# Attention with head mixing on one core: T's place and A become two tiles, and the first two units' odd heads are sent from ScalarE's queue

## The chip, the cores and the metric

One core of a Trainium2 chip runs the whole program. The metric is the device time of one execution in microseconds, as the median of three runs. The engines go by the names of the profile: PE (TensorE), with PEld its weight loads, DVE (VectorE), ACT (ScalarE), POOL (GpSimd) and SP (SyncE, which here only begins transfers).

## What is computed

An attention layer whose heads are mixed before and after the softmax, and behind it a dense layer with a gated activation.

```python
scores = scale * np.matmul(q, k.transpose(0, 1, 3, 2))       # 4 batches, 12 heads, 448 x 448, head size 64
scores = np.einsum('bhij,hg->bgij', scores, w_pre)
scores = scores - np.max(scores, axis=-1, keepdims=True)
attn = np.exp(scores)
attn = attn / (np.sum(attn, axis=-1, keepdims=True) + 1e-09)
attn = np.einsum('bhij,hg->bgij', attn, w_post)
x = np.matmul(attn, v)                                       # to (1792, 768)
h = x @ w_in                                                 # to (1792, 2048)
g = h * np.clip(h + 3.0, 0.0, 6.0) / 6.0
out = g @ w_out                                              # to (1792, 768)
```

## The kernel before

Query rows are worked through in 32 units of 60 rows, eight to a batch (the last of a batch holds fewer). One unit `m` goes through these stations:

- **Scores.** PE multiplies queries by keys for two pairs of heads at a time (L432, `p` = 0, 1, 2). The result is copied from PSUM to a tile `s`: by ACT in one piece (L457), or in the first two units by ACT for the even heads and by DVE for the odd ones (L454, L455).
- **Regrouping.** Mixing heads on PE needs the heads along the partitions. So for each head one transfer (L464) takes its 60 rows of 448 numbers from `s` to a tile `T`, as 10 partitions times 6 rows, 105 KB. A unit has twelve. All are begun on SP's queue. `T` of the even units lies in the columns 0 to 5375 of a large tile `AR`, that of the odd units in a tile of its own, `T_one`.
- **Steps.** Three steps a unit, each with up to 20 query rows: mix before the softmax (PE, L521), row maximum (DVE, L529), exponent with row sum (ACT, L530), a small sum on POOL (L532) and its reciprocal on DVE (L533), normalisation (POOL, L539), the split of a number into two halves of 16 bits (ACT, L541, and POOL, L542), and the mix after the softmax (PE, L558). Its two PSUM results go to `A`, one by ACT (L569) and one by DVE (L567). `A` is the part of `AR` from column 6144 on, a ring of three units.
- **Values.** PE multiplies `A` by the values (L603), and ACT and DVE write `x` (L608, L609).
- **Dense layer, first half.** L801 with the activation L814 and L816, for every group of 240 or 208 rows; `g` goes to memory and comes back later. The weights are read and decoded meanwhile: `w_in` by L649 to L719 from transfers of 768 KB (L341), `w_out` likewise.
- **Phase B.** When attention is done, `AR` is used again for weights and for `g` of the second half (L898, L899; two slots of 11520 columns, `wg`), and the products L1071 run to the end.

The order of all this on each engine is drawn up by a planner in the kernel (`Plan`). Every operation is entered with its engine, a planned duration, what it reads and writes and a due time. The planner plays the program through with these durations, for several small variations of the due times, keeps the shortest and emits the instructions in that order. Where PE has a planned gap between 9 and 150 us it puts in multiplications of no use (`filler`, L839), to keep the clock up. The planner treats `T` and `A` as separate buffers. The waits between engines come from elsewhere: the framework records which tiles an instruction touches and puts in semaphore waits for them. Transfers take turns on eight semaphores, so that each also waits for the landing of the one eight places earlier; the rows of order below name these DMAHW0 to DMAHW7.

Of the kernel before, what the change touches and what calls it, by code (L numbers as in the profile page):

```python
# [11 lines left out]
F16 = mybir.dt.float16  # L12
BF16 = mybir.dt.bfloat16
F32 = mybir.dt.float32
# [9 lines left out]
B, H, S, D = 4, 12, 448, 64  # L24
DM, FF = 768, 2048
NT = B * S
P = 128
# [4 lines left out]
CU = 60  # L32
# [259 lines left out]
def body(ctx: ExitStack, tc: tile.TileContext, q4, kT, vj, wpre0, wpost0, ident0, w_in, w_out, outT):  # L292
    nc = tc.nc
    PE, ACT, DVE, POOL, SP = nc.tensor, nc.scalar, nc.vector, nc.gpsimd, nc.sync
# [4 lines left out]
    apool = ctx.enter_context(tc.tile_pool(name="apool", bufs=1))  # L299
# [9 lines left out]
    plan = Plan()  # L309
# [3 lines left out]
    def buf(pool, shape, dt, tag, name, bufs=1, ring=True):  # L313

        g = rings.setdefault((id(pool), tag), Ring(bufs)) if ring else None
        return Buf(lambda: pool.tile(shape, dt, tag=tag, name=name, bufs=bufs), g)

    def const(shape, dt, name, pool=keep):
        return Buf(lambda: pool.tile(shape, dt, name=name))

    def act(dur, fn, r, w, prio):
        return plan.op("ACT", dur, fn, r, w, prio)

    def dve(dur, fn, r, w, prio, share=False):
        return plan.op("DVE", dur, fn, r, w, prio, share=share)
# [4 lines left out]
    def pe(dur, fn, r, w, prio, after=(), mode=0):  # L330
        return plan.op("PE", dur, fn, r, w, prio, after, 0, mode)

    def dma(nbytes, fn, r, w, prio, after=()):
        return plan.op("SP", 0.5, fn, r, w, prio, after, nbytes)
# [22 lines left out]
    def place(places):  # L357
        z = Buf(None)
        z.pool = places
        return z  # L360
# [50 lines left out]
        qs[b, c] = t  # L411
        (bulk if b + c else dmas)(P * QX * 4, t, q4[b, c], [t], at, after)

    AR = const([P, 23424], F16, "AR", apool)
    T_one = const([P, 6, S], F32, "T_one", one)
    T_home = [lambda: AR()[:, :5376].bitcast(F32).rearrange("p (t j) -> p t j", t=6), T_one]
    T_zero = [Buf(None), T_one]
    a_ring = Ring(3)
    last_qk, last_av, Ts, Au = [], [], {}, {}

    def a_view():
        return AR()[:, 6144:].bitcast(F32).rearrange("p (x y) -> p x y", y=3 * CU)

    def products(q, half, ks_, p, at):

        def mm():
            for cc in range(2):
                pr = 2 * p + cc
                o = (6 * half + pr) * CU
                for u in range(2):  # L430
                    r = slice(u * D, u * D + D)
                    PE.matmul(at[u]()[cc * D:cc * D + D], q()[r, o:o + D], ks_[cc]()[r, pr % 3, :], start=True, stop=True)  # L432

        return mm

    def scores(m, p, at):
        b, n = divmod(m, 8)
        c, half = divmod(n, 2)
        if p == 0:
            Ts[m] = Buf(T_home[m % 2], rings.setdefault(("T", m % 2), Ring(1)))  # L440
        T, q = Ts[m], qs[b, c]
        ks_ = [ks[b, (2 * p + cc) // 3] for cc in range(2)]
        kr = [(ks_[cc], (2 * p + cc) % 3) for cc in range(2)]
        st = buf(wpool, [P, 2, S], F32, "x", f"s_{m}_{p}", X_BUFS) if m == 0 else buf(rot, [P, 2, S], F32, "s", f"s_{m}_{p}", 2)
        if m < 2 and (m or p):
            ps = [place(singles) for u in range(2)]
            at2 = [lambda u=u: ps[u]()[:, :S] for u in range(2)]
        else:
            two = place(pairs)
            ps = [(two, 0), (two, 1)]  # L450
            at2 = [lambda u=u: two()[:, u, :S] for u in range(2)]
        last_qk[:] = [pe(0.77, products(q, half, ks_, p, at2), [*kr, q], ps, at, last_qk, mode=1)]
        if m < 2:
            act(0.48, lambda: ACT.activation(st()[:, 0], at2[0](), AF.Copy), [ps[0]], [(st, 0)], at + 0.5)  # L454
            dve(0.57, lambda: DVE.tensor_copy(st()[:, 1], at2[1]()), [ps[1]], [(st, 1)], at + 0.5)  # L455
        else:
            act(0.9, lambda: ACT.activation(st(), two()[:, :, :S], AF.Copy), ps, [(st, 0), (st, 1)], at + 0.5)  # L457
        parts = [(0, 10, 6, 0)] if n < 7 else [(0, 10, 2, 0), (20, 5, 2, 2)]
        for cc in range(2):
            for u in range(2):  # L460
                h = 2 * (2 * p + cc) + u
                for q0, r, t, t0 in parts:
                    def go(cc=cc, u=u, h=h, q0=q0, r=r, t=t, t0=t0):
                        SP.dma_start(T()[4 + h:4 + h + 12 * (r - 1) + 1:12, t0:t0 + t], st()[D * cc + q0:D * cc + q0 + r * t, u, :])  # L464

                    dma(r * t * 2100, go, [(st, u), T_zero[m % 2]], [(T, (h, t0))], at + 0.7)


    vs = {}
# [32 lines left out]
    def step(s):  # L502
# [31 lines left out]
        if t == 0:  # L534
            Au[m] = Buf(a_view, a_ring)
# [312 lines left out]
    for m in range(2):  # L848
        for p in range(3):
            scores(m, p, -10 + 8 * m + 1.6 * p)  # L850
# [6 lines left out]
    for s in range(NS + 12):  # L857
# [5 lines left out]
        while todo and todo[0][0] - 2 <= s:  # L863
            at, m, p = todo.pop(0)
            if p == 0 and m % 2 == 0:
                queries(m // 8, m % 8 // 2, at - 5)
            scores(m, p, at)
# [13 lines left out]
        for C in range(16):  # L881
            b, c = divmod(C, 4)
# [28 lines left out]
    def minus(out, x, y, op, at, big, after=()):  # L911
        plan.op("DVE", 1.15, lambda: DVE.tensor_tensor(out(), x(), y(), op=op), [x, y], [out], at, after, share=True)

    WS, GP = {}, {}
    wg_ring = Ring(2)

    def wg(i):
        return Buf(lambda: AR()[:, 11520 * i:11520 * i + 11520], wg_ring)

    slots = [wg(i) for i in range(2)]  # L920
    t_last, a_last = last_pre[-5:-2], last_av[-4:]

    def w_view(t, z, i):
        return t()[:, :6144].rearrange("p (z m f c) -> p z m f c", z=2, m=3, f=8)[:, z, i // 2, 4 * (i % 2):4 * (i % 2) + 4]

    def g_view(t, at, z):
        return t()[:, at:at + 1792].rearrange("p (z f n) -> p z f n", z=2, f=4)[:, z]

    WS["P1"] = slots[0]

    def w_split(name, i, t, at, after):
        b = WS[name]
        split(View(t, lambda: t().rearrange("p (f c) -> p f c", f=4)), wo_r[int(name not in ("P1", "P2"))], lambda y: w_view(b, y, i), (b, (name, i)), 4 * P, at, after, False)

    def g_split(name, b, i, t, x, o, at, after):
        GP[name, b, i] = (lambda z: g_view(x, o, z)), (x, (name, b, i))
        split(t, g_s[b], lambda z: g_view(x, o, z), (x, (name, b, i)), 4 * NH, at, after, True)
# [69 lines left out]
    def g_tile(name):  # L1007
        return gbuf([P, 4, NH], F32, "gr", name, GR)

    def g_load(b, kk, half, i, at):  # L1010
        t = g_tile(f"g{kk}{half}_{b}_{i}_{at}")
        src, keys_ = g_rows(b, kk, half, i)
        load(458752, lambda: SP.dma_start(t(), src()), keys_, [t], at, [close_a])
        return t

    def g_put(name, b, i, t, at, home):
        after = [close_a]
        if home is None:
            ring = later_home.pop(0) if name not in ("P1", "P2") and later_home else "gx"
            if ring == "gy":  # L1020
                after = [close_a, close_w]
            x = gbuf([P, 1792], F16, "gx", f"gx_{name}_{b}_{i}", GX) if ring == "gx" else wbuf([P, 1792], F16, "gy", f"gy_{name}_{b}_{i}", GY)
            home = x, 0
        x, o = home
        g_split(name, b, i, whole(t), x, o, at, after + (a_last if x is slots[1] else []))
# [10 lines left out]
    def g_two(b, at):  # L1036
        later_home[:] = ["gy"] * GY
        if b % 2:
            z = [wg(i) for i in range(2)]
        for i in range(2):  # L1040
            t = at + (6 if b else G2_BY) * i
            b12, b11, b22, b21 = g_load(b, 0, 1, i, t), g_load(b, 0, 0, i, t + 0.1), g_load(b, 1, 1, i, t + 0.2), g_load(b, 1, 0, i, t + 0.3)
            t1 = g_tile(f"t1_{b}_{i}")
            minus(t1, b12, b11, ALU.subtract, t + 1, True)
            minus(b11, b22, t1, ALU.subtract, t + 1.1, True)
            minus(b12, b22, b12, ALU.subtract, t + 1.2, True)
            minus(b21, b21, b11, ALU.subtract, t + 1.3, True)
            for j, (name, x) in enumerate((("P6", b11), ("P7", b12), ("P4", b21), ("P5", t1), ("P3", b22))):
                home = None
                if b % 2:  # L1050
                    n = 5 * i + j
                    home = z[n // 5], 1792 * (n % 5)
                g_put(name, b, i, x, t + 2 + j, home)

    u_t = {}
# [78 lines left out]
    for b in range(B):  # L1134
        g_two(b, 2000 + 1000 * b if b else G2_AT)
        stage2(b, 20000 + 1000 * b)
# [54 lines left out]
```

## Time and profile before

| | us |
|---|---|
| median of three runs | 926.43 |
| lowest, highest | 920.86, 934.22 |
| profiled execution | 935.05 |
| its span, first to last instruction | 933.3 |
| PE busy, of the span | 838.6 (90%) |
| DVE, ACT, POOL busy | 602.5, 529.7, 373.1 |
| mean granted clock of PE | 0.936 |

The profile is of one execution. Busy time of PE is modelled at the ends of matmuls, and a matmul at the lower clock is busy for longer. A wait for several semaphores is put down to the one that came last.

### The profile page before, as it was taken

How to read it: one execution, taken by the hardware profiler on the slowest of the kernel's cores; microseconds unless marked ns; L12 is line 12 of the kernel's file. 1: busy time of each engine (PE TensorE's matmuls, PEld its weight loads, DVE VectorE, ACT ScalarE, POOL GpSimd, SP SyncE). 2: the span in 40 equal slices, each digit the busy share in tenths (PEclk: the TensorE clock that was granted, in tenths of full speed). 3: DMA queues.
4: the chain of work that ended last, by engine and by line, in shares of the span. 5: the costliest groups of instructions: out<-in, count | busy, mean ns of one | idle time of the engine just before them, and what ended most of it. 6: DMA issues, size and time to landing. Idle time of an engine off the chain costs nothing.

```text
span 933.3 us, 28114 instructions
## 1 busy us (share of the span) xinstructions
PE 838.6 (90%) x11599; PEld 661.4 (71%) x11599; DVE 602.5 (65%) x1185; ACT 529.7 (57%) x1043; POOL 373.1 (40%) x535
## 2 busy tenths in 40 slices
PE   8699997698798898898897898889899999999998
PEld 2356665455475675676575666567799999999998
DVE  4477584458565734877565597586457588898542
ACT  3357685467676755676666666678447475243110
POOL 3145686267774744565545446668200000000000
PEclk9779699789999998999988999899999999999999
DMA  6563543362534465554645656553449785463301
GB/s 211 187 188 119 157 137 120 93 216 92 176 104 132 120 203 185 173 176 144 196 122 188 199 178 199 173 159 92 122 131 356 221 264 173 124 185 113 100 25 46
DMA packets 100417, 146.98 MB, mean 157 GB/s; under 512 B 9824, under 2 KB 79552, under 8 KB 100288
## 3 DMA queue, kind: packets, MB, share of 16 engines
q1 hardware_dynamic: 100288, 145.17, 50.1%
q8 instruction: 91, 1.49, 0.7%
q14 instruction: 38, 0.31, 0.1%
HBM read 75.23 MB, written 31.20 MB: 114 GB/s over the span
## 4 chain that ended last, share of the span: by engine, by line
PE 51%; DMA 12%; DVE 10%; ACT 8%; SPq 7%; POOL 6%; issue 5%; ACTq 0%; DVEq 0%; POOLq 0%
PE single L1071 21%; PE single L801 13%; SPq L464 6%; DMA AR<-s 6%; PE single L558 5%; PE pair L432 4%; PE single L521 3%; POOL e L539 3%; DVE nb L529 3%; POOL el L542 3%; PE single L603 2%; ACT e L530 2%; ACT s L457 2%; DMA T_one<-s 2%; DMA wsd_P<-WF 2%
## 5 line engine op out<-in xcount | busy, mean ns | idle before, releaser
L801 PEld LDWEIGHTS <-wi 128*128 128x128 f16 x2304 | 217.3, 99 | 37.1 <-issue 28.9
L801 PE MATMUL single<-x,wi 128*128 128x208 f16 (+1 forms) x2304 | 233.3, 263 | 9.4 <-ACT AR L569 6.6
L542 POOL TENSOR_TENSOR el<-e,eh 128x448 f16<-128x448 f32 x156 | 172.3, 1119 | 87.9 <-ACT eh L541 85.6
L539 POOL TENSOR_SCALAR e<-e,r 128x448 f32<-128x448 f32 x180 | 132.2, 746 | 77.1 <-DVE r L533 69.7
L1071 PEld LDWEIGHTS <-ws_P 128*128 128x128 f16 x1440 | 138.0, 98 | 0.0
L530 ACT ACTIVATE e<-single,nb 128x448 f32<-128x448 f32 x180 | 113.0, 637 | 35.2 <-DVE nb L529 34.9
L432 PE MATMUL pair<-ks,qx 64*64 64x448 f32 x728 | 101.6, 627 | 27.7 <-ACT s L457 27.3
L567 DVE TENSOR_SCALAR AR<-single 128x480 f32<-128x480 f32 (+1 forms) x92 | 58.4, 641 | 95.6 <-DMA AR<-s 68.7
L529 DVE TENSOR_REDUCE nb<-single 128x1 f32<-128x448 f32 x180 | 102.5, 613 | 21.9 <-PE single L521 21.6
L569 ACT ACTIVATE AR<-single 128x480 f32<-128x480 f32 (+1 forms) x92 | 52.9, 582 | 100.1 <-DMA AR<-s 66.5
L457 ACT ACTIVATE s<-pair 128x896 f32<-128x896 f32 x90 | 82.3, 915 | 37.6 <-DMA T_one<-s 20.6
L541 ACT ACTIVATE eh<-e 128x448 f16<-128x448 f32 x156 | 87.0, 576 | 19.8 <-POOL e L539 18.7
L814 ACT ACTIVATE g<-single,three,uh 128x240 f32<-128x240 f32 (+1 forms) x128 | 68.2, 540 | 51.6 <-PE single L801 51.2
L603 PEld LDWEIGHTS single<-AR,v 128*64 128x64 f32 x1536 | 80.6, 144 | 22.5 <-DVE AR L567 6.3
L558 PEld LDWEIGHTS <-eh 60*128 60x128 f16 x2496 | 69.2, 101 | 34.4 <-issue 31.2
L603 PE MATMUL single<-AR,v 128*64 128x120 f32 (+1 forms) x1536 | 86.1, 273 | 6.6 <-DVE AR L567 6.2
L816 DVE SCALAR_TENSOR_TENSOR g<-g,six,single 128x240 f32<-128x240 f32 (+1 forms) x128 | 56.3, 442 | 53.4 <-ACT g L814 53.1
L558 PE MATMUL single<-wpost_h,eh 60*128 60x60 f16 x1248 | 76.6, 204 | 11.1 <-ACT e L530 5.4
L558 PE MATMUL single<-wpost_h,el 60*128 60x60 f16 x1248 | 75.6, 204 | 4.4 <-POOL el L542 4.4
L558 PE MATMUL single<-wpost_l,eh 60*128 60x60 f16 x1248 | 75.4, 204 | 0.0
L1071 PE MATMUL single<-gx_P,ws_P 128*128 128x224 f16 x720 | 69.3, 259 | 0.0
L1071 PE MATMUL single<-AR,ws_P 128*128 128x224 f16 x720 | 69.3, 259 | 0.0
(241 smaller groups left out, 1163.8 us busy)
## 6 DMA issues: line engine op xcount, KB each, us to landing
AR<-s SPq DMA_DIRECT2D x192, 105.0 KB
T_one<-s SPq DMA_DIRECT2D x144, 105.0 KB
wi<-in_w_in SPq DMA_DIRECT2D x16, 768.0 KB
wo<-in_w_out SPq DMA_DIRECT2D x24, 512.0 KB
wsd_P<-WF SPq DMA_DIRECT2D x42, 256.0 KB
wP<-wsd_P SPq DMA_DIRECT2D x36, 256.0 KB
gd<-g SPq DMA_DIRECT2D x32, 240.0 KB
gd<-g SPq DMA_DIRECT2D x32, 208.0 KB
```

Of the source, the lines that this page charges most:

```text
L432: PE.matmul(at[u]()[cc * D:cc * D + D], q()[r, o:o + D], ks_[cc]()[r, pr % 3, :], start=True, stop=True)
L457: act(0.9, lambda: ACT.activation(st(), two()[:, :, :S], AF.Copy), ps, [(st, 0), (st, 1)], at + 0.5)
L529: dve(0.53, lambda r=r: DVE.tensor_reduce(nb()[:, r:r + 1], ps[r]()[:, :S], axis=AX.X, op=ALU.max, negate=True), [ps[r]], [(nb, r)], s + 0 ...
L530: act(0.62, lambda r=r: ACT.activation(e()[:, r], ps[r]()[:, :S], AF.Exp, bias=nb()[:, r:r + 1], accum_out=sm()[:, r:r + 1]), [ps[r], (nb, ...
L539: pool(0.63, lambda r=r: POOL.tensor_scalar(e()[:, r], e()[:, r], rr()[:, r:r + 1], 1.0, op0=ALU.mult, op1=ALU.mult), [rr], [(e, r)], s + ...
L541: act(0.47, lambda r=r: ACT.activation(eh()[:, r], e()[:, r], AF.Copy), [(e, r)], [(eh, r)], s + 0.65 + 0.3 * r)
L542: pool(1.02, lambda r=r: POOL.tensor_tensor(el()[:, r], e()[:, r], eh()[:, r], op=ALU.subtract), [(e, r), (eh, r)], [(el, r)], s + 0.7 + 0 ...
L558: PE.matmul(out, x()[rows, r, js], z()[rows], start=(i == 0), stop=(i == len(mix) - 1))
L603: PE.matmul(ps()[u * D:(u + 1) * D, k:k + (n if p1 else CI)], v()[:, jc, g * D:(g + 1) * D], cols(jc * H + g), start=(jc == 0), stop=(jc = ...
L801: PE.matmul(pv(), wi_g[g]()[:, w, f0, cc, :], x()[:, z, cc, :n], start=(cc == 0 and i == 0), stop=(cc == 5 and i == 2))
L814: act(0.44, lambda fc=fc, pv=pv, r=r: ACT.activation(r(), pv(), AF.Relu, bias=three()[:, fc:fc + 1], scale=uh()[:, fc:fc + 1]), [ps, (thre ...
L1071: PE.matmul(ps()[:, :NH], w_view(w, y, 2 * m + i)[:, f], g(x)[:, f, :], start=(i == 0 and f == 0 and (y, x) == (0, 0)), stop=(i == 1 and f ...
```

## The change

The tile `AR` of 23424 columns becomes two: `AR` of 17280 and `T_two` of 6144 columns. `T` of the even units moves to `T_two`, and `A` begins at column 0 of `AR`. In phase B the two slots are put together from pieces of these tiles: slot 0 has its weights in `T_two` and its `g` in the first 5376 columns of `AR`, slot 1 has both in the rest of `AR`. `w_view`, `g_view` and the place of `g` in `g_two` follow from that. Besides, the transfers of the odd heads (`u` = 1) of units 0 and 1 are begun on ACT's queue, and every transfer of this line is entered into the plan with 0.8 us in place of 0.5.

```diff
-    AR = const([P, 23424], F16, "AR", apool)
+    AR = const([P, 17280], F16, "AR", apool)
+    T_two = const([P, 6144], F16, "T_two", apool)
     T_one = const([P, 6, S], F32, "T_one", one)
-    T_home = [lambda: AR()[:, :5376].bitcast(F32).rearrange("p (t j) -> p t j", t=6), T_one]
+    T_home = [lambda: T_two()[:, :5376].bitcast(F32).rearrange("p (t j) -> p t j", t=6), T_one]
...
     def a_view():
-        return AR()[:, 6144:].bitcast(F32).rearrange("p (x y) -> p x y", y=3 * CU)
+        return AR()[:, :].bitcast(F32).rearrange("p (x y) -> p x y", y=3 * CU)
...
                     def go(cc=cc, u=u, h=h, q0=q0, r=r, t=t, t0=t0):
-                        SP.dma_start(T()[4 + h:4 + h + 12 * (r - 1) + 1:12, t0:t0 + t], st()[D * cc + q0:D * cc + q0 + r * t, u, :])
-
-                    dma(r * t * 2100, go, [(st, u), T_zero[m % 2]], [(T, (h, t0))], at + 0.7)
+                        (ACT if m < 2 and u else SP).dma_start(T()[4 + h:4 + h + 12 * (r - 1) + 1:12, t0:t0 + t], st()[D * cc + q0:D * cc + q0 + r * t, u, :])
+
+                    plan.op("ACT" if m < 2 and u else "SP", 0.8, go, [(st, u), T_zero[m % 2]], [(T, (h, t0))], at + 0.7, (), r * t * 2100)
...
     def wg(i):
-        return Buf(lambda: AR()[:, 11520 * i:11520 * i + 11520], wg_ring)
+        return Buf(lambda: (AR()[:, 5376:11520], AR()[:, 11520:16896]) if i else (T_two(), AR()[:, :5376]), wg_ring)
```

The lines of the program move down by one from L413 on (L464 is L465 after, L567 is L568, L569 is L570, L521 is L522, L603 is L604, L839 is L840). In the rows of order, a name in brackets is a semaphore that the instruction waits for: PE, DVE, Activation and Pool are engines, DMAHW0 to DMAHW7 the landing of transfers.

DVE, around the first of its copies to `A` (`single` is the PSUM result of L558, `vst` a maximum over values, `WF` a decoded block of `w_in`). Before:

```order
L344 TENSOR_REDUCE vst_0_339<-v_0_266 128x1 [waits DMAHW0_49]
L567 TENSOR_SCALAR AR_96<-single5_156 128x48x10 [waits DMAHW4_49,DMAHW5_49,DMAHW3_49,DMAHW6_49,DMAHW2_49,DMAHW7_49,DMAHW0_49,PE_49]
L533 RECIPROCAL r_4_375<-sm_4_337 128x2 [waits Pool_49]
L652 TENSOR_SCALAR WF_194,wist_1_380<-WF_194 128x768 [waits Activation_49]
L567 TENSOR_SCALAR AR_96<-single2_139 128x48x10 [waits PE_49]
```

After:

```order
L534 RECIPROCAL r_2_299<-sm_2_246 128x2 [waits Pool_49]
L665 SCALAR_TENSOR_TENSOR WF_223<-wi_0_118,WF_223 128x768 [waits DVE_49]
L568 TENSOR_SCALAR AR_305<-single2_139 128x48x10 [waits PE_49]
L344 TENSOR_REDUCE vst_0_267<-v_0_218 128x1 [waits DMAHW2_49]
L534 RECIPROCAL r_4_332<-sm_4_294 128x2 [waits Pool_49]
```

The first copy names seven landings before and PE alone after. Over the whole program 36 of DVE's 92 copies and 33 of ACT's 92 name a landing before, and none after.

ACT at the start of the program, from its first copy of scores on. Before:

```order
L454 ACTIVATE s_0_0_127<-pair0_120 128x448 [waits PE_49]
L454 ACTIVATE s_0_1_141<-single0_85 128x448 [waits PE_49]
L454 ACTIVATE s_0_2_161<-single3_145 128x448 [waits PE_49]
L454 ACTIVATE s_1_0_182<-single5_156 128x448 [waits PE_49]
L454 ACTIVATE s_1_1_190<-single1_131 128x448 [waits DVE_49,PE_49]
L649 ACTIVATE WF_194<-wi_0_118 128x768 [waits DMAHW1_49]
```

After:

```order
L455 ACTIVATE s_0_0_127<-pair0_120 128x448 [waits PE_49]
L465 DMA T_two_96<-s_0_0_127 10x6x448 [waits DMAHW2_49,DVE_49]
L465 DMA T_two_96<-s_0_0_127 10x6x448 [waits DMAHW4_49]
L455 ACTIVATE s_0_1_151<-single0_85 128x448 [waits PE_49]
L455 ACTIVATE s_0_2_161<-single3_145 128x448 [waits PE_49]
L465 DMA T_two_96<-s_0_1_151 10x6x448 [waits DMAHW6_49,DVE_49]
L465 DMA T_two_96<-s_0_1_151 10x6x448 [waits DMAHW0_49]
L465 DMA T_two_96<-s_0_2_161 10x6x448 [waits DMAHW2_49,DVE_49]
L465 DMA T_two_96<-s_0_2_161 10x6x448 [waits DMAHW4_49]
```

Two and then four transfers of unit 0 stand between ACT's copies; those of unit 1 follow in the same way.

SP at the same place, from the load of the first block of `w_in` (`wi_0`, on the semaphore DMAHW1) on. Before:

```order
L341 DMA wi_0_118<-in_w_in 128x768 [waits DMAHW1_49]
L464 DMA AR_96<-s_0_0_127 10x6x448 [waits DMAHW2_49,Activation_49]
L464 DMA AR_96<-s_0_0_127 10x6x448 [waits DMAHW3_49]
L464 DMA AR_96<-s_0_0_127 10x6x448 [waits DMAHW4_49,DVE_49]
L464 DMA AR_96<-s_0_0_127 10x6x448 [waits DMAHW5_49]
L464 DMA AR_96<-s_0_1_141 10x6x448 [waits DMAHW6_49,DVE_49]
L464 DMA AR_96<-s_0_1_141 10x6x448 [waits DMAHW7_49]
L464 DMA AR_96<-s_0_1_141 10x6x448 [waits DMAHW0_49,Activation_49]
L464 DMA AR_96<-s_0_1_141 10x6x448 [waits DMAHW1_49]
```

After:

```order
L341 DMA wi_0_118<-in_w_in 128x768 [waits DMAHW1_49]
L465 DMA T_two_96<-s_0_0_127 10x6x448 [waits DMAHW3_49,Activation_49]
L465 DMA T_two_96<-s_0_0_127 10x6x448 [waits DMAHW5_49]
L465 DMA T_two_96<-s_0_1_151 10x6x448 [waits DMAHW7_49,Activation_49]
L465 DMA T_two_96<-s_0_1_151 10x6x448 [waits DMAHW1_49]
L465 DMA T_two_96<-s_0_2_161 10x6x448 [waits DMAHW3_49,Activation_49]
L465 DMA T_two_96<-s_0_2_161 10x6x448 [waits DMAHW5_49]
L341 DMA qx_0_2_194<-in_q4 128x724 [waits DMAHW7_49,PE_49]
```

Of twelve transfers of unit 0 six are left on SP; the fourth of them now waits for the semaphore that `wi_0` uses, which before was the wait of the eighth.

## Rows read from the trace of the kernel before

**Rows 1.** The page: busy us, share of the span; granted clock in 40 slices (tenths).

```profile
PE 838.6 (90%) x11599; PEld 661.4 (71%) x11599; DVE 602.5 (65%) x1185; ACT 529.7 (57%) x1043; POOL 373.1 (40%) x535
PEclk9779699789999998999988999899999999999999
```

**Rows 2.** Stretches: start:end, length, busy us of each engine, clock, DMA share, GB/s.

```profile
12.00:700.00 688.00, 597.88 (x9127) 428.22 (x9121) 440.23 (x937) 435.47 (x913) 367.82 (x526) 0.91 0.50 154
700.00:755.00 55.00, 55.00 (x587) 54.30 (x586) 37.89 (x64) 34.22 (x56) 0.33 (x2) 1.00 0.90 292
```

**Rows 3.** Waits: engine, tile, line, releaser; us in total, times, longest.

```profile
DVE AR L567 <- DMA AR<-s: 68.7, 18, 13.5
ACT AR L569 <- DMA AR<-s: 66.5, 20, 10.9
PE pair L432 <- ACT s L457: 27.3, 15, 4.6
PE single L521 <- DMA T_one<-s: 4.2, 3, 2.5
```

**Rows 4.** Waits of SP's queue at L464, the four largest.

```profile
SPq L464 <- DVE AR L567: 37.9, 18, 5.5
SPq L464 <- ACT eh L541: 26.2, 21, 4.2
SPq L464 <- PE single L521: 23.7, 11, 4.6
SPq L464 <- ACT e L530: 22.9, 22, 3.4
```

**Rows 5.** The chain that ended last: shares of the span by line.

```profile
by line: PE single L1071 20.7%; PE single L801 13.0%; SPq L464 6.5%; DMA AR<-s 6.2%; PE single L558 5.2%; issue 5.1%; PE pair L432 4.3%; PE single L521 3.4%; POOL e L539 2.8%; DVE nb L529 2.6%; POOL el L542 2.5%; PE single L603 2.4%; ACT e 
```

**Rows 6.** Timeline, 28 to 40 us: start, length, engine, line; idle before and releaser.

```profile
27.90 2.00 PE L558 MATMUL single<-wpost_n,e 60*128 60x60 f32 x32
...
28.04 3.69 SPq L464 DMA_DIRECT2D AR<-s  x4
...
37.93 0.59 ACT L569 ACTIVATE AR<-single 128x480 f32<-128x480 f32 x1 [8.53 <-DMA AR<-s]
37.94 0.66 DVE L567 TENSOR_SCALAR AR<-single 128x480 f32<-128x480 f32 x1 [6.00 <-DMA AR<-s]
...
39.45 0.90 PE L558 MATMUL single<-wpost_n,e 60*128 60x60 f32 x6 [6.54 <-POOL e L539]
```

**Rows 7.** Stretches: 4 of the 18 around the waits of rows 3, and all.

```profile
29.40:42.90 13.50, 6.91 (x78) 5.99 (x76) 5.36 (x10) 2.63 (x4) 2.70 (x5) 0.75 0.59 204
...
156.00:177.90 21.90, 12.10 (x175) 8.27 (x173) 5.09 (x13) 7.33 (x14) 6.42 (x10) 0.61 0.42 134
...
457.30:473.40 16.10, 10.57 (x166) 5.26 (x159) 7.04 (x12) 6.40 (x14) 3.85 (x6) 0.68 0.32 98
546.50:555.10 8.60, 7.24 (x102) 2.68 (x94) 6.83 (x14) 4.02 (x9) 3.48 (x5) 0.80 0.38 121
...
sum 195.10, PE 147.90 PEld 103.00 DVE 102.70 ACT 103.85 POOL 89.53; mean PE 8.22 PEld 5.72 DVE 5.71 ACT 5.77 POOL 4.97
```

**Rows 8.** Timeline, 0 to 20 us, the first unit's way to L521.

```profile
6.61 0.54 ACT L454 ACTIVATE s<-pair 128x448 f32<-128x448 f32 x1 [4.60 <-PE pair L432]
...
7.18 10.03 SPq L464 DMA_DIRECT2D AR<-s  x12
7.19 0.62 DVE L455 COPY s<-pair 128x448 f32<-128x448 f32 x1 [0.74 <-ACT s L454]
...
12.96 0.91 ACT L649 ACTIVATE WF<-wi 128x768 f32<-128x768 f32 x1 [1.48 <-DMA wi<-in_w_in]
...
19.52 0.98 PE L521 MATMUL single<-AR,wpre 64*64 64x448 f32 x8 [1.27 <-DMA T_one<-s]
```

**Rows 9.** Groups of instructions on PE: count, busy us, mean ns, idle before.

```profile
L801 PE MATMUL single<-x,wi 128*128 128x208 f16 (+1 forms) x2304 | 233.3, 263 | 9.4 <-ACT AR L569 6.6 <-ACT e L530 2.0 <-DVE AR L567 0.8
...
L839 PE MATMUL single<-ident 128*128 128x512 bf16 x63 | 18.3, 434 | 0.1
```

More of the change, by code (lines that the diff above doesn't have):

```diff
@@ L923, in w_view @@
     def w_view(t, z, i):
-        return t()[:, :6144].rearrange("p (z m f c) -> p z m f c", z=2, m=3, f=8)[:, z, i // 2, 4 * (i % 2):4 * (i % 2) + 4]
+        x = t()
+        return (x[0] if isinstance(x, tuple) else x[:, :6144]).rearrange("p (z m f c) -> p z m f c", z=2, m=3, f=8)[:, z, i // 2, 4 * (i % 2):4 * (i % 2) + 4]
     def g_view(t, at, z):
-        return t()[:, at:at + 1792].rearrange("p (z f n) -> p z f n", z=2, f=4)[:, z]
+        x = t()
+        if isinstance(x, tuple):
+            x, at = x[at // 6144], at % 6144
+        return x[:, at:at + 1792].rearrange("p (z f n) -> p z f n", z=2, f=4)[:, z]
     WS["P1"] = slots[0]
@@ L1051, in g_two @@
                     n = 5 * i + j
-                    home = z[n // 5], 1792 * (n % 5)
+                    home = z[n // 5], 1792 * (n % 5) + (768 if n % 5 > 2 else 0)
                 g_put(name, b, i, x, t + 2 + j, home)
```

## The prediction

> **What bounds the kernel now.** I read the page first: the matrix engine (PE) is busy 838.6 of 933.3 us, and the line of its granted clock has its low tenths in the first half of the span [rows 1]. The table of stretches splits this: from 700 us on PE has no gap at full clock (55.00 of 55.00), while from 12 to 700 us it is busy 597.88 of 688.00 at a mean clock of 0.91 [rows 2]. So the last 233 us are PE's own work, and what a change can win lies before 700: 90.1 us of PE gaps, and the work done at the lower of its two levels (1.2 instead of 2.4 GHz).
>
> Next the list of waits. ACT and DVE copy each finished block of A out of PSUM (L569, L567, 92 times each). These copies should wait only for PE, yet 18 on DVE and 20 on ACT were released last by a transfer into AR, the tile that also holds T of the even units: 68.7 and 66.5 us [rows 3]. They share no byte: T is columns 0 to 5375, A starts at 6144. The same holds the other way: transfers of T into AR wait 37.9 us on SP's queue for DVE's copies to A [rows 4]. In the chain that ended last, transfers into AR are 6.2% (58 us) and SP's queue at L464 6.5% (61 us) [rows 5], so these waits do reach the end.
>
> One case in full [rows 6]: PE ends the first block at 29.9; four transfers of the next even unit's T start at 28.04, and the copies run only at 37.93 and 37.94. ACT had stood 8.53 us and DVE 6.00, and PE, whose next operand waits for DVE's reciprocal behind that copy, had a gap of 6.54 us.
>
> **The change, part by part.**
>
> (a) *T and A in two tiles.* Of the 184 copies 69 name landings of transfers before and none after (order rows of DVE); of 192 transfers into the even T 35 name DVE before; after, only the producers of s, PE's reads and the queue's own lanes remain. No instruction is added. What is it worth? Not 135 us: ACT and DVE mostly stand at once, and a late copy costs time only when PE runs dry. I laid the 37 listed waits over each other, added 5 us behind each for PE to feel it, and got 18 stretches of 195.1 us together, with PE busy 147.90: 47.2 us of gaps [rows 7]. The other 492.9 us before 700 hold 90.1 − 47.2 = 42.9 us of gaps, 0.087 per us. At that rate the 195.1 us would still have 17.0, because the next producer (exponent, normalisation, split) is then the late one. Gain 47.2 − 17.0 = **30.2 us**; bounds 0 (all gaps come back under another name) and 87.5 (the union of the waits themselves, all on the path).
>
> (b) *The clock behind these gaps.* Length times (1 − clock) over the 18 stretches is 23.7 us: 3.4, 8.5, 5.2 and 1.7 in the four rows shown, 4.9 in three others [rows 7]. All 688 us have 688 × 0.09 = 62 [rows 2], so elsewhere it is 38 in 492.9, or 15.2 in 195.1 us. The difference, 8.5, counts only while PE works, 147.9/195.1 of the time: **6.4 us**; bounds 0 and 23.7 × 0.76 = 18.
>
> (c) *Twelve transfers begun on ACT.* Before, SP begins the twelve of unit 0 back to back: 10.03 us from 7.18 to 17.21, some 0.8 each, and the first mix (L521) starts at 19.52, 2.3 later [rows 8]. After (order rows of ACT and SP), ACT copies until 7.15, waits for DVE's copy (7.81), begins two (9.4), makes two copies of 0.54 (10.5) and begins four (13.7). SP begins two, waits for the copy on ACT (10.0), begins one, waits at the second for the lane of the first w_in block, which lands just before 12.96, and begins three: 15.4. The last start moves from 17.2 to 15.4: **1.9 us**. The price on ACT, six starts of 0.8 us among its copies, is in this count; unit 1's six follow, 4.8 us of ACT in front of the first exponents, at a time when ACT before had little to do. Bounds: those 4.8 lost, and 4.8 won if SP's other six are all that is left.
>
> Here a page speaks against me. The Trainium skill, "DMA: Bandwidth & Descriptors", Issuing engines are not separate DMA queues, says that transfers begun on several engines share the same 16 DMA engines, and that only the issue time is saved, usually small next to the transfer. By its main clause (c) is 0 and the sum 41.1 instead of 43.0. The trace has the starts in one unbroken row of 10.03 us, so here the issue time is the path.
>
> (d) *What stood behind T on SP.* A transfer into AR that waits for DVE holds SP's later ones: T_one of the odd units, then the copy of s (L457), then PE's score products, whose gaps behind L457 are 27.3 us [rows 3]. Of the four largest causes of SP's waits at L464 (37.9, 26.2, 23.7, 22.9) [rows 4] DVE's copy is a third; a third of 27.3 is 9.1, and I take half as already in (a): **4.5 us**; bounds 0 and 27.3.
>
> (e) *The planner.* It now reckons 0.8 us on SP for each start at L465 where it had 0.5, so the whole order is drawn anew. In PE's order the warming matmuls at L839, which only fill planned gaps, fall from 63 (18.3 us [rows 9]) to 38, and 1944 instead of 1800 of the 2304 products of L801 stand before the last L603: more work inside the stage with gaps, less behind it, PE's sum the same. I take 0. Bounds: half of the missing fillers' 18.3 × 25/63 = 7.3, some 4 us lost, if the lower clock takes their place; and 15 us won, 144 products at 233.3 / 2304 = 0.101 us each [rows 9], if all of them fall into gaps (which is mostly (a) again).
>
> (f) *Phase B.* Weights of slot 0 lie in T_two, its g in AR, slot 1 in AR with another offset. The same instructions; PE has no gap there to cover or lose [rows 2]. 0.
>
> Sum: 30.2 + 6.4 + 1.9 + 4.5 = 43.0. The profiled execution took 935.05 us (span 933.3), so 892.0. The three timed runs are 920.86 to 934.22 with median 926.43, below the profiled one by a factor of 0.9908: 892.0 × 0.9908 = **884**.
>
> **The rivals.**
>
> *All of it was on the path.* Then the union, 87.5 us, goes: (935.05 − 87.5) × 0.9908 = 840. For it: the chain's 58 us of transfers into AR plus 61 us of SP's queue. Against: in the union PE was still busy on work already queued, and POOL, ACT and DVE wait for one another at every step.
>
> *T is simply late.* Once the copy no longer waits, the mix L521 waits for the same transfers, and (a) and (b) return as PE gaps. Left are (c) and (d): 935.05 − 6.4 = 928.7, times 0.9908 is 920. For it: at 28.04 the transfers truly take some 9 us to land. Against: PE's direct waits for T at L521 are 4.2 us in three cases [rows 3], since scores run a unit ahead.
>
> *The new order is worse.* With T's starts dearer by 0.3 us, some 420 × 0.3 = 126 us more of planned SP time, the planner may put the scores later, so that T lands after its first step is due. There are 31 such hand-overs. At 1.4 us each the 43 us are gone; from 2.0 us each the kernel is slower by over 2%; at 2.2 it is near 951. Against: in PE's order the scores of unit 2 stand after 12 products of L521 instead of 20, and later units within a step of where they were.
>
> **How the numbers follow.** Forecast 0.72, with its own range 866 to 910; all on the path 0.10; T late 0.13; worse order 0.05. About 2% is what a measurement of this kernel can tell from no change: under 907.9 is faster, over 945.0 slower. Faster: the first rival, and all of the forecast but 0.02: 0.80. Slower: 0.04 of the last. Within: 0.16. The range 856 to 914 takes the forecast, the slow edge of the first rival and the fast edge of the second, about 8 in 10.
>
> **What would show it.** (a) L568 and L570 with no idle behind a transfer, PE busy over 625 of the 688 us from 12 to 700, or the same work ending earlier. (b) A mean clock of 0.92 or more there. (c) First L522 at 17.3 to 18.0 us. (d) SP's waits at L465 for DVE gone, PE's gaps behind L458 under 23 us. The forecast falls if gaps of the same sum appear at L522 behind transfers into T_two (T late), or if the stage before the last L604 ends no earlier though those waits are gone.

## The result, and the profile after

The changed kernel takes 837.25 us (833.23 to 841.37, four runs) against 927.13 before: a ratio of 0.903, with a 95% interval of 0.895 to 0.911. The way was forecast, the size was not: 90 us went, 43 were predicted, and the time lies below the stated range. The profiled execution of the kernel before was one of its slowest, 8 us above the median of 927, so differences between its trace and another are too large by up to about as much.

The page of the profiled execution (837.03 us, span 835.2), the lines that answer to [rows 1]: busy time of PE and the granted clock.

```profile
PE 795.4 (95%) x11574; PEld 639.6 (77%) x11574; DVE 599.0 (72%) x1185; ACT 531.2 (64%) x1043; POOL 375.4 (45%) x535
PEclk9799899989999999999999999999999999999999
```

PE stands still for 835.2 − 795.4 = 39.8 us where it did for 94.7, so 54.9 us of gaps are gone. Its busy time is 43.2 us less, though it does the same useful work: 8.7 of that is filler (18.3 to 9.6 us), the other 34.5 is the same work done in less time. The mean granted clock rose from 0.936 to 0.977: 933.3 × 0.064 = 60 us of clock were lost before, 835.2 × 0.023 = 19 now. The gaps and the busy time make the 98.1 us between the spans. The stretches, as in [rows 2], show that PE has no gap from 600 us on, not from 700, and where the rest of the gaps is:

```profile
12.00:600.00 588.00, 553.65 (x9042) 405.94 (x9035) 426.26 (x914) 431.15 (x906) 368.52 (x519) 0.97 0.58 177
600.00:655.00 55.00, 55.00 (x644) 53.89 (x641) 43.07 (x82) 38.91 (x61) 1.27 (x8) 1.00 0.81 259
```

The waits that answer to [rows 3]: the copies to A now wait for PE alone, and PE waits little for the copy of the scores.

```profile
ACT AR L570 <- PE single L559: 8.8, 22, 1.3
ACT s L458 <- DMA T_two<-s: 8.6, 6, 4.4
DVE AR L568 <- PE single L559: 6.8, 11, 1.8
ACT s L458 <- DMA T_one<-s: 6.6, 8, 1.8
PE single L522 <- DMA T_one<-s: 6.5, 1, 6.5
PE pair L433 <- ACT s L458: 5.5, 9, 1.6
```

On SP's queue DVE's copies, first in [rows 4], are no longer among the causes; the three largest:

```profile
SPq L465 <- PE single L522: 18.5, 9, 7.6
SPq L465 <- ACT e L531: 14.8, 21, 1.5
SPq L465 <- ACT eh L542: 11.3, 14, 1.8
```

The start went another way than worked out. Timeline, as in [rows 8] (at L522 the profile names a transfer into T_one as releaser, though the mix reads T_two; releasers are inferred):

```profile
6.82 8.45 SPq L465 DMA_DIRECT2D T_two<-s  x6
...
7.49 2.21 ACTq L465 DMA_DIRECT2D T_two<-s  x2
...
10.67 4.73 ACTq L465 DMA_DIRECT2D T_two<-s  x3
...
15.38 0.57 SPq L341 DMA_DIRECT2D qx<-in_q  x1
...
16.38 3.67 ACTq L465 DMA_DIRECT2D T_one<-s  x3
...
20.07 5.37 PE L522 MATMUL single<-T_two,wpre 64*64 64x448 f32 x24 [6.50 <-DMA T_one<-s]
```

The last start of unit 0 ends at 15.40. That is the number computed, but in part by luck: it was computed for SP, which ends at 15.27, and for ACT 13.7 was computed, where ACT ends at 15.40. The first mix begins at 20.07, half a microsecond later than before.

### The profile page after: what moved, and what is told of

Its sections match the earlier page's. It is cut to its first block, busy times and chain, and to the rows that moved or that the text cites. A ratio compares the mean times of both kernels' runs of the same rounds, so it can differ in the third digit from the quotient of the medians.

```text
span 835.2 us, 27976 instructions
## 1 busy us (share of the span) xinstructions
PE 795.4 (95%) x11574; PEld 639.6 (77%) x11574; DVE 599.0 (72%) x1185; ACT 531.2 (64%) x1043; POOL 375.4 (45%) x535
## 4 chain that ended last, share of the span: by engine, by line
PE 59%; DMA 13%; ACT 9%; DVE 7%; SPq 5%; POOL 4%; issue 2%; ACTq 0%; DVEq 0%; POOLq 0%
PE single L1076 23%; PE single L802 15%; PE single L604 6%; PE single L559 5%; DMA T_two<-s 5%; PE single L522 5%; PE pair L433 5%; SPq L465 4%; DMA T_one<-s 4%; ACT e L531 3%; POOL el L543 2%; DMA v<-in_vj 2%; ACT s L458 2%; POOL e L540 1%; ACT eh L542 1%
## 5 line engine op out<-in xcount | busy, mean ns | idle before, releaser
L802 PE MATMUL single<-x,wi 128*128 128x208 f16 (+1 forms) x2304 | 227.7, 259 | 2.6 <-ACT e L531 2.6
L802 PEld LDWEIGHTS <-wi 128*128 128x128 f16 x2304 | 213.3, 98 | 19.2 <-issue 12.8
L540 POOL TENSOR_SCALAR e<-e,r 128x448 f32<-128x448 f32 x180 | 134.6, 758 | 36.5 <-DVE r L534 32.9
L530 DVE TENSOR_REDUCE nb<-single 128x1 f32<-128x448 f32 x180 | 102.5, 613 | 25.5 <-PE single L522 25.2
L433 PE MATMUL pair<-ks,qx 64*64 64x448 f32 x728 | 94.2, 574 | 5.9 <-ACT s L458 5.5
L458 ACT ACTIVATE s<-pair 128x896 f32<-128x896 f32 x90 | 82.2, 913 | 26.5 <-PE pair L433 9.8
L604 PEld LDWEIGHTS single<-AR,v 128*64 128x64 f32 x1536 | 75.5, 137 | 12.7 <-issue 3.0
L604 PE MATMUL single<-AR,v 128*64 128x120 f32 (+1 forms) x1536 | 81.2, 264 | 0.7 <-ACT e L531 0.7
L533 POOL TENSOR_SCALAR sm<-sm 128x2 f32<-128x2 f32 (+1 forms) x92 | 23.5, 255 | 126.5 <-ACT e L531 120.5
L559 PEld LDWEIGHTS <-el 60*128 60x128 f16 x1248 | 65.5, 102 | 4.1 <-POOL el L543 4.1
L568 DVE TENSOR_SCALAR AR<-single 128x480 f32<-128x480 f32 (+1 forms) x92 | 57.9, 639 | 7.2 <-PE single L559 6.8
```

Source lines behind the costliest of these rows:

```text
L530: dve(0.53, lambda r=r: DVE.tensor_reduce(nb()[:, r:r + 1], ps[r]()[:, :S], axis=AX.X, op=ALU.max, negate=True), [ps[r]], [(nb, r)], s + 0 ...
L540: pool(0.63, lambda r=r: POOL.tensor_scalar(e()[:, r], e()[:, r], rr()[:, r:r + 1], 1.0, op0=ALU.mult, op1=ALU.mult), [rr], [(e, r)], s + ...
L559: PE.matmul(out, x()[rows, r, js], z()[rows], start=(i == 0), stop=(i == len(mix) - 1))
L604: PE.matmul(ps()[u * D:(u + 1) * D, k:k + (n if p1 else CI)], v()[:, jc, g * D:(g + 1) * D], cols(jc * H + g), start=(jc == 0), stop=(jc = ...
L802: PE.matmul(pv(), wi_g[g]()[:, w, f0, cc, :], x()[:, z, cc, :n], start=(cc == 0 and i == 0), stop=(cc == 5 and i == 2))
```

## The experiments

Two things had to be told apart. The change takes waits away, and it draws up a new order, because another duration is in the plan and another queue is used. The planner treats T and A as separate buffers in every version, so the tiles do not enter its order: a kernel with the split alone has the order of the kernel before, one with the rest of the change alone has that of the changed kernel, and each differs from it in waits alone. The traces show the same sequence on every engine in both pairs, but for four positions on PE.

The first four edits are shown against the changed kernel, in the lines that matter.

**Only the split** (order of before):

```diff
-    (ACT if m < 2 and u else SP).dma_start(...)
-    plan.op("ACT" if m < 2 and u else "SP", 0.8, go, ...)
+    SP.dma_start(...)
+    plan.op("SP", 0.5, go, ...)
```

> Only the tiles are split: transfers all on SP, planned at 0.5 us, so the order on every engine is that of the kernel before and only waits differ. Theory W (the waits between T and A were on the path, all of them, in any order): 835 to 850 us, near the changed kernel's 837. Theory O (the new order and the two queues at the start carry a good part of the 90 us): 870 to 895 us, the sum of the prediction without its second part being 886.

Measured: 869.05 us (866.10 to 870.82), ratio 0.938 (0.934 to 0.942). Just below the band of theory O, 19 us above that of theory W. The split alone takes 57.6 us off; 32 more come with the order.

**Only the new order** (T and A in one tile):

```diff
-    AR = const([P, 17280], F16, "AR", apool)
-    T_two = const([P, 6144], F16, "T_two", apool)
+    AR = const([P, 23424], F16, "AR", apool)
```

> Only the second part of the change: odd heads of units 0 and 1 from ACT's queue, 0.8 us planned, T and A still in one tile. The order on every engine is that of the changed kernel, only waits differ from it. Theory W: 915 to 940 us, as before. Theory O: 870 to 895 us. If the new order meets the old waits worse than the old order did: over 945 us.

Measured: 930.08 us (924.11 to 935.89), ratio 1.003 (0.999 to 1.007). The new order by itself gives nothing. In that order, then, the waits cost 93 us; in the old one 58.

**Split, 0.8 us, all on SP** (first line), and **split, ACT's queue, 0.5 us** (second):

```diff
+    plan.op("SP", 0.8, go, ...)
...
+    plan.op("ACT" if m < 2 and u else "SP", 0.5, go, ...)
```

> Tiles split, planned at 0.8 us, but all transfers on SP. Theory W: 835 to 850 us. If the two queues at the start matter beyond their price: 845 us or more, first mix not before 19.5 us. If they cost more than they give: 830 to 836 us.

Measured: 818.62 us (814.15 to 820.66), ratio 0.883 (0.879 to 0.887): faster than the changed kernel, without the second queue, and with its first mix at 21.45 us, later than in either.

> Tiles split, odd heads of units 0 and 1 on ACT's queue, but planned at 0.5 us. Theory W: 835 to 850 us, whatever the number in the plan. If the planned 0.8 us (nearer to the 0.75 to 0.8 that a start takes in the trace) makes the order better: 845 to 860 us here.

Measured: 851.27 us (850.68 to 856.67), ratio 0.921 (0.916 to 0.926). So in these first orders the number in the plan matters, on either queue. Theory W, by which the order is worth nothing, falls with the first and the third; theory O, by which it is worth much by itself, with the second. What is left is that the waits hid what the order is worth.

**The fourth corner: one tile, SP, 0.8 us.** The kernel before with `plan.op("SP", 0.8, go, ...)`.

> T and A still in one tile, all transfers on SP, planned at 0.8 us: the fourth corner beside the kernel before (0.5 us, one tile), the split at 0.5 us (869) and the split at 0.8 us (818.6). Theory M (the waits between T and A mask what a better order is worth): 915 to 940 us, as before. Theory S (the order is worth its 50 us by itself, and the sum of parts holds): 870 to 885 us.

Measured: 909.34 us (908.28 to 910.75), ratio 0.980 (0.975 to 0.984). Below the band of theory M, but nearer to it: the step from 0.5 to 0.8 is worth 18 us with one tile and 50 with two. Here is where it went. The waits of the copies to A in this kernel, the longest first:

```profile
ACT AR L569 <- DMA AR<-s: 105.9, 27, 9.1
DVE AR L567 <- DMA AR<-s: 93.5, 26, 8.8
```

and in the one-tile kernel with the changed order:

```profile
ACT AR L569 <- DMA AR<-s: 108.6, 29, 8.2
DVE AR L567 <- DMA AR<-s: 80.6, 24, 6.9
```

199 and 189 us, where the order of before has 135 [rows 3]. At the same time the copy of the scores hardly waits for transfers any more. In the kernel before:

```profile
ACT s L457 <- DMA T_one<-s: 20.6, 10, 4.8
```

and in these two, in the same order, 0.2 and 0.9 us behind T_one and 3.9 and 1.7 behind the transfers into AR. One wait went and the other grew.

**Is it the number, or the luck of a draw?** The planner keeps the best of its 32 draws by its own reckoning; other draws give another order in detail.

```diff
-        for k in range(TRIALS):
+        for k in range(1000, 1000 + TRIALS):
```

> The split, all on SP, 0.8 us in the plan, but the planner draws 32 other variations of the due times, so that the order differs in detail. Theory D (0.8 us is better because it is near the true price of a start): 812 to 832 us again. Theory L (818.6 was one lucky order; orders scatter by some 15 us each way): anywhere from 820 to 865 us.

Measured: 825.63 us (823.16 to 829.79), inside the bands of both theories.

> The split, all on SP, 0.5 us in the plan, 32 other variations. Theory D: 858 to 880 us, near the 869 of the first draw. Theory L: anywhere from 820 to 880 us, and not clearly behind the second draw at 0.8 us.

Measured: 846.29 us (837.63 to 851.07), below theory D's band: at 0.5 us the draw alone moved the time by 23 us. But it is 21 us behind the second draw at 0.8 us, where theory L had no clear difference.

> A third draw of the split, all on SP, 0.8 us. The first two gave 818.6 and 825.6. Theory D: 812 to 835 us.

Measured: 826.04 us (819.37 to 829.96). The third draw begins at 2000.

**Other numbers in the plan**, all on SP, first draw: 0.65 and 1.0 us.

> The split, all on SP, 0.65 us in the plan, half way. Theory D (the nearer the plan is to the 0.75 to 0.8 us of a start in the trace, the better): 830 to 848 us, between the 846 to 869 at 0.5 and the 819 to 826 at 0.8. Theory L (scatter of orders alone): no tie to the number, anywhere from 815 to 870 us.

Measured: 842.15 us (841.27 to 845.33), inside the bands of both theories.

> The split, all on SP, 1.0 us in the plan, more than a start takes. Theory D: not better than 0.8 us, 818 to 840 us. If any reserve on SP's queue helps: below 815 us. Theory L: anywhere from 815 to 870 us.

Measured: 838.58 us (837.06 to 849.27). More than a start takes is no better, in this one order.

**The two queues**, other draws of the changed kernel:

> The changed kernel with 32 other variations. If the transfers on ACT's queue cost 18 us by themselves (837.3 against 818.6): 830 to 850 us, clearly behind the second draw with all on SP. If that difference was the scatter of orders: within 8 us of the second draw on SP, on either side.

Measured: 820.26 us (814.74 to 822.86), 5 us ahead of the same draw on SP.

> A third draw of the changed kernel, with the two queues. The first two gave 837.3 and 820.3. If the two queues cost time by themselves: at least 8 us behind the third draw on SP, and the mean of three behind by 8 or more. If they neither cost nor give: the means of three within 8 us.

Measured: 819.82 us (815.45 to 827.78), 6 us ahead of its partner.

Together, with the tiles split (ACT's column has the odd heads of units 0 and 1 on its queue). The fourth column is the idle time of ACT before its copy of the scores (L458) that a transfer into T ended, summed over T_one and T_two, in the order of the times beside it. The last is the number of the 2304 products of L802 that stand before the last L604, counted in each trace:

| us in the plan | all on SP | odd heads on ACT | ACT's copy waits for transfers into T | L802 before the last L604 |
|---|---|---|---|---|
| 0.5 | 869.1, 846.3 | 851.3 | 29.3, 27.5; 25.9 | 1800, 2016; 1944 |
| 0.65 | 842.2 | | 25.2 | 1944 |
| 0.8 | 818.6, 825.6, 826.0 | 837.3, 820.3, 819.8 | 5.1, 12.9, 7.1; 15.2, 9.3, 8.1 | 2016, 1944, 1944; 1944, 2016, 2016 |
| 1.0 | 838.6 | | 6.2 | 2016 |

The medians of the six at 0.8 us (mean 824.6) lie all below those of the three at 0.5 (mean 855.5): 31 us, and no overlap. Part of the scatter goes with the last column: at 0.8 us the three orders with 2016 products lie below the three with 1944, by 10 us on average. It does not make the 31 us: with 1944 products in both, 0.8 is 22 us ahead of 0.5, and with 2016 in both 27. The two queues make no difference that stands out from the draws: 823.4 (all on SP) and 825.8 on average.

The tile `s` has two buffers, so that a copy of new scores must wait until the transfers have read the old ones; ACT works in order, and everything behind that copy waits too. For the split at 0.5 us (first draw):

```profile
ACT s L458 <- DMA T_one<-s: 21.1, 13, 4.1
PE pair L433 <- ACT s L458: 15.7, 16, 2.9
ACT s L458 <- DMA T_two<-s: 8.2, 6, 2.7
```

and for the split at 0.8 us, all on SP, the same three pairs:

```profile
ACT s L458 <- DMA T_two<-s: 3.5, 3, 1.8
ACT s L458 <- DMA T_one<-s: 1.6, 2, 0.8
PE pair L433 <- ACT s L458: 1.1, 2, 0.7
```

PE's line of the page in that kernel (span 815.5 us):

```profile
PE 795.8 (98%) x11634; PEld 641.6 (79%) x11634; DVE 601.4 (74%) x1185; ACT 530.8 (65%) x1043; POOL 375.3 (46%) x535
```

Twelve starts take 10.03 us [rows 8]. A planner that reckons 0.5 believes them done in 6 us, and puts ACT's copy where the transfers have not yet read its buffer. At 0.8 these waits are between 5 and 15 us in all six orders, and the best has 815.5 − 795.8 = 19.7 us of gaps left. That the wait goes with the number is shown in eleven orders. That it makes the whole of the 31 us is not: PE's gaps behind this copy (the line `PE pair L433 <- ACT s L458`) are 13.7 us on average at 0.5 and 4.4 at 0.8, while all of PE's gaps fall from 51.1 to 29.9. So 9 of these 21 us are PE waiting for the copy itself; what the copy delays behind it on ACT may make more of them, which is argued only. At 1.0 the wait stays small and the time does not, so there another price is paid, which stays open.

## Why the prediction was wrong, step by step

**What bounds the kernel** held: after the last value product (L603, L604) PE's gaps come to at most 0.5 us in every version but one, with 2.4, and what was won is won before it.

**(a) The split: right, and right in size where it was looked for.** Split-only and before run the same 11599 matmuls on PE in the same order (four positions differ), so every stretch of the one can be found in the other by its first and last matmul. The 18 stretches around the waits, 195.1 us long with 47.2 us of gaps [rows 7], are 151.2 us long in split-only, and PE is busy for 137.26 of them (first two and sum of the table of stretches):

```profile
32.00:41.50 9.50, 9.50 (x76) 8.01 (x76) 3.77 (x7) 2.73 (x4) 1.25 (x2) 0.50 0.59 199
76.90:83.70 6.80, 6.80 (x107) 5.35 (x108) 3.98 (x9) 4.64 (x7) 3.20 (x6) 1.00 0.40 139
...
sum 151.20, PE 137.26 PEld 98.34 DVE 103.93 ACT 106.46 POOL 90.69; mean PE 7.63 PEld 5.46 DVE 5.77 ACT 5.91 POOL 5.04
```

13.9 us of gaps are left where I expected 17.0, so 33.3 went where I expected 30.2: here the subtraction by the rate elsewhere held. The largest of them, before, at 157 to 175 us:

```profile
160.63 1.77 PE L432 MATMUL pair<-ks,qx 64*64 64x448 f32 x8 [3.60 <-ACT s L457]
...
169.51 0.66 DVE L567 TENSOR_SCALAR AR<-single 128x480 f32<-128x480 f32 x1 [13.53 <-DMA AR<-s]
...
170.22 5.07 PE L603 MATMUL single<-AR,v 128*64 128x120 f32 x48 [6.20 <-DVE AR L567]
```

The same matmuls in split-only (timeline, 146 to 160 us):

```profile
150.35 1.77 PE L433 MATMUL pair<-ks,qx 64*64 64x448 f32 x8 [2.89 <-ACT s L458]
...
153.53 2.68 PE L604 MATMUL single<-AR,v 128*64 128x120 f32 x48
```

The value products follow the scores by 3.2 us instead of 9.6, with no gap before them, and they run in 2.68 us instead of 5.07. Only the copy of the scores ahead of them is nearly as late as before.

**(b) The clock: too small.** Split-only has the same matmuls with nearly the same filler (18.3 and 17.4 us), so its busy time tells what the waits had cost besides gaps:

```profile
PE 812.7 (94%) x11599; PEld 652.4 (75%) x11599; DVE 603.4 (70%) x1185; ACT 530.1 (61%) x1043; POOL 374.7 (43%) x535
```

838.6 − 812.7 − 0.9 = 25.0 us, where I had 6.4 and a bound of 18. Inside the 18 stretches it is 147.9 − 137.3 = 10.6, so over half of it, some 14, lies outside. Not all of it is the clock. Set side by side, matmul by matmul, with the clock that each trace grants at that time, the matmuls at different clocks in the two make 17.1 of it, 6.8 inside the stretches of before and 10.3 outside; matmuls at full clock in both make 7.4, most of it in the mixes (L521, L522): eight matmuls that take 0.93 us in split-only, four at a time, were staggered in pairs before and took 1.37. So inside the stretches the clock came out. The step that failed is the subtraction of 15.2 us and the edge of the stretches: what the clock lost elsewhere I took for a background that no stall of this kind had made, and dropped. Split-only has a mean clock of 0.965 over its span, so 865.7 × 0.035 = 30 us of lost clock, where before has 60 (the 62 of the prediction comes of the rounded 0.91). All of it lies before the end of the stage:

```profile
12.00:620.00 608.00, 559.97 (x9004) 407.87 (x8998) 433.99 (x926) 430.34 (x906) 369.43 (x526) 0.95 0.56 171
```

Some 29 went, more than the 23.7 that lay in the stretches at all. By the mean clocks of all timed executions (0.942 over thirteen of before, 0.968 over four of split-only) it is 26.

**(c) The two queues: the last start came out, in part by luck, the landing did not.** The last start ended at 15.40, the number worked out, though on the other queue. I let the landing take 2.3 us as before; from 15.40 to the first mix are 4.7 us. In the trace a load of queries starts at 15.38 and transfers of unit 1 on both queues from 15.56 on, so that more is under way at once. In the third draw with two queues the load of queries starts only at 18.39, and the way is still 3.7 us; that the second queue is the cause is not shown. The page of the Trainium skill that I had weighed against the term ("DMA: Bandwidth & Descriptors", Issuing engines are not separate DMA queues) was right for the time of the kernel: three draws with and three without the second queue differ by 2.4 us on average. The first mix itself did come earlier than in the draws at 0.8 us on SP alone: 20.07, 19.56 and 19.60 against 21.45, 21.82 and 21.52. But it is no bound here: the fastest kernel has it at 21.45 us, 1.4 later than the changed one.

**(d) SP's queue: between 2.7 and 8.4 us for 4.5.** All gaps fell by 94.7 − 53.0 = 41.7 us, 33.3 of them in the stretches, so 8.4 outside. PE's wait for the copy of the scores fell from 27.3 [rows 3] to 15.7 us, but mostly inside the stretches, where (a) counts it; outside it fell from 13.0 to 10.3. The size fits; that SP's queue is what gave the 8.4 us is not shown.

**(e) The planner: the step with the largest miss.** I set the new order to 0, from the counts of filler and of early L801 products, and looked at 0.8 only as a danger. It is 0 to 18 us as long as T and A share a tile (930 and 909 against 927), and 31 us on average, 32 in the changed kernel, once they do not. The step that failed is that I gave the order no worth: 0, with 15 us as the most that the 144 products moved forward could bring, where it brought 32; how much of the 32 these products made is not shown. Both numbers were before me: the planned 0.5 and the measured 0.8 us a start. Terms were added that depend on each other: the transfers' lateness was paid at the copies to A as long as these waited for them, wherever the planner put the rest.

**(f)** held: no gap in the last stage of the changed kernel.

Summed up, between the profiled executions of before and of split-only, the split gave 41.7 us of gaps and 25.0 of busy time where (a), (b) and (d) had 41.1 for both; by the medians it gave 57.6. The other 32 us of the 90 are (e).

**The rivals.** "All of it was on the path" gave 840 us and came near for the wrong reason: the split alone brought 57.6 us, not the union of 87.5. "T is simply late" did not come about: PE's waits for T at L522 are 8.5 us, most of them the first mix. "The new order is worse" was tried alone: 930 us, no difference.

## What to carry to other kernels

Gaps that a removed wait leaves can be counted stretch by stretch, less the rate of gaps elsewhere; the clock can't be counted so, since it is lost behind the stretch as well: here 25 us of busy time came back with 42 us of gaps, 17 of them by the clock. What a planned order is worth hangs on its durations, and a false wait elsewhere can hide it; after one bottleneck is removed, measure the planner's numbers again. An order that a search drew up should be judged over several draws, since one draw against another moved the time by up to 23 us here.

## What was not expected of the hardware

A transfer's way from start to landing was not a constant: the last of unit 0's transfers was followed by the first mix 2.3 us after its start ended before, and 4.7 us after it with two queues in use. In split-only, with one queue, it is 2.2, and in the other two draws with two queues 3.6 and 3.7.

A stall on PE was paid a second time in the work behind it, which ran at the lower clock (1.2 GHz in place of 2.4). The 48 value products that took 5.07 us before and 2.68 us in split-only stand in these two stretches (before, then split-only; the clock is the number ahead of the last two), the first behind a gap of 6.20 us:

```profile
170.20:175.30 5.10, 5.08 (x52) 4.78 (x54) 2.78 (x9) 2.43 (x6) 1.31 (x2) 0.50 0.14 39
```

```profile
153.50:156.30 2.80, 2.80 (x59) 2.63 (x61) 2.62 (x8) 2.41 (x5) 1.75 (x6) 1.00 0.83 241
```
